# Tiles that matmuls take weights from, padded and moved to multiples of 128 bytes of SBUF

## The chip, the core and the metric

The kernel runs on one NeuronCore of one Trainium2 chip. The metric is the device time of one execution in microseconds (us). Engines are named as in the profile: PE is TensorE (its weight loads stand apart as PEld), DVE VectorE, ACT ScalarE, POOL GpSimd, SP SyncE, whose queue issues most DMAs. SBUF is the on-chip memory with 128 partitions; an offset here is a tile's start address within a partition, modulo 128 bytes.

## What is computed

Three stages run on x of shape (4, 3072, 256), all in float32: a two-dimensional Fourier transform of which the real part is kept, a gated network whose gate mixes all 3072 tokens of a batch, and a second gated network on the 12288 tokens.

```python
x = np.fft.fft(np.fft.fft(x, axis=1), axis=2).real          # (4, 3072, 256)
h = np.maximum(x @ w_in, 0.0)                                # (4, 3072, 1024)
u, v = h[..., :512], h[..., 512:]
v_n = (v - mean(v)) / sqrt(var(v) + 1e-6)                    # over the last axis
v_s = einsum('ts,bsd->btd', w_spatial, v_n) + b_spatial      # (3072 x 3072) per batch
x = ((u * v_s) @ w_out).reshape(12288, 256)
gate = 1 / (1 + exp(-(x @ w_gate)))                          # (12288, 1536)
out = (gate * (x @ w_val)) @ w_out2                          # (12288, 256)
```

## The kernel before

Every product of float32 numbers is made of three matmuls. An operand is split into a high part in the matmul's format float32r and a low part, the rest; `mm3` (lines 256 to 258) issues high x high, high x low and low x high (weights first) into the same PSUM bank. Each of the three has weights of 128 x 128 (the `lhsT` operand, which a weight load brings into the array) and streams 384, 386 or 512 columns of the other operand past them.

- **Transform stage** (to about 310 us). The Fourier transform along the tokens is folded by its symmetries and done as matmuls of folded samples (weights fh, fl, fohl) with cosine and sine tables c1, c2, c3 (streamed), into psf. ACT and DVE take the result into the pairs ph and pl (`take_fft`, line 421). The Fourier transform along the channels and the product with w_in are one product with gc (tiles gh and gl of the pool `keep`) and g3: `v_block` takes weights from ph, pl and nt and streams gc, into psv; `u_block` takes weights from gc and g3 and streams ph, pl and nt, into psu. v is normalized and stored to HBM as v_d, u as u_d. A plan by steps (FOLDS, SPLITS, AT3 and the others) sets the order.
- **Strassen stage** (to about 1827 us). The mixing over tokens runs as Strassen's scheme of seven products, for two pairs of batches and three column blocks: 42 leaves. A leaf is a loop of 6 x 2 x 4 `mm3` with weights from vh, vl and streams from wh, wl, all in pools on the left side of SBUF. DVE and ACT prepare the next tiles three steps ahead (`advance`). DVE takes the four banks into the sums C (`evacuate`), and where a product completes a result it forms the gate g, splits it into gh and gl (here tiles of the pool `gp`), and `second` multiplies that with w_out: two blocks of 12 matmuls, weights woh and wol, streams gh and gl.
- **Gated stage** (to the end). 12 pairs of token blocks by 12 feature blocks, 144 groups. A group forms seven Strassen products with weights wgh, wgl (in the left pools; wg is one tile with both parts) and streams from x tiles: the first seven in the left pool (x0 to x6), then also tail and x7 in tiles of the pool `cp`. `outputs` multiplies the gated result, again tiles gh and gl of `gp`, by weights wv, which lie in `cp`. The order within a group is written by hand: `p12` of group n, `outputs` of n-2, `p34` of n-1, `p67`, `outputs` again, `p5`.

What decides the offsets is the order of allocation. The pools `keep`, `pqp`, `tmp`, `stp`, `vp`, `up` (transform stage), then `cp` and `gp` (later stages) grow from the right end of SBUF toward the left, each below the one before, and a tile is rounded up to a multiple of 32 bytes. `keep` begins with the 28 bytes of masks (line 315), and nt3 has 386 columns, 1544 bytes. The left pools begin at offset 0 and hold tiles of multiples of 128 bytes where matmuls take weights.

```python
masks = keep.tile([P, 3 + B], F32, name="masks")                                                # 315
nts = [keep.tile([P, R3 if unit == 3 else H], F32R, name=f"nt{unit}") for unit in range(4)]     # 318
nn = R3 if q == 0 else H                                                                        # 422
fn = tmp.tile([P, 4, 3 * B], F32, name="fn")                                                    # 480
nt = stp.tile([P, R3], F32R, tag="nt", name="nt", bufs=1)[:, : R3 if unit == 3 else H]          # 588
C = [[cp.tile([P, 4, 512], F32, tag=f"c{k}{c}", name=f"c{k}{c}") for k in range(2)] for c in range(3)]  # 1148
```

Of the kernel before, what the change touches and what calls it, by code (L numbers as in the profile page):

```python
# [9 lines left out]
F32 = mybir.dt.float32  # L10
F32R = mybir.dt.float32r
# [8 lines left out]
B, S, D = 4, 3072, 256  # L20
# [4 lines left out]
P = 128  # L25
H = 384
R3 = H + 2
NT_TOK = B * S


# [13 lines left out]
def _trig(f, num, den):  # L44

    return f(2.0 * np.pi * (np.asarray(num, np.int64) % den) / den)
# [28 lines left out]
def _constants():  # L75
# [15 lines left out]
    c2q = _trig(np.sin, r[:, None] * (2 * i + 1)[None], S // 2)  # L91
    c3p = _trig(np.cos, r[:, None] * np.arange(R3)[None], S // 4)
    c3p[:, H + 1] = 0.0
# [10 lines left out]
def _special_constants():  # L104
# [5 lines left out]
    q2 = _trig(np.sin, s[:, None] * (2 * (2 * j + 1))[None], S)  # L110
    p3 = _trig(np.cos, s[:, None] * (4 * np.arange(R3))[None], S)
    p3[:, H + 1] = 0.0
# [6 lines left out]
SP_P1, SP_Q1, SP_Q2, SP_P3 = 0, H, 2 * H, 3 * H  # L119
SP_N = 3 * H + R3  # L120

# [113 lines left out]
def tile_kernel(ctx: ExitStack, tc: tile.TileContext, t: dict, out: bass.AP):  # L235
# [10 lines left out]
    def f(ap):  # L246
        return ap.bitcast(F32)
# [51 lines left out]
    def pool(stack, name, bufs, side="left", **kw):  # L299
        return stack.enter_context(tc.tile_pool(name=name, bufs=bufs, side=side, reuse_waits="tile", **kw))  # L300
# [3 lines left out]
    keep = pool(r0, "keep", 1, "right")  # L304
# [7 lines left out]
    ps_l = pool(ps0, "ps_l", 1, space=PSUM)  # L312
    ps_w = pool(ps0, "ps_w", 6, space=PSUM)

    masks = keep.tile([P, 3 + B], F32, name="masks")
    gc = [keep.tile([P, 2, DFF], F32R, name=f"g{n}") for n in "hl"]
    g3 = keep.tile([P, DFF], F32R, name="g3")
    nts = [keep.tile([P, R3 if unit == 3 else H], F32R, name=f"nt{unit}") for unit in range(4)]
    sps = cst.tile([P, B + 1, 2, P], F32R, name="sps")
    spc = cst.tile([P, SP_N], F32R, name="spc")  # L320
    cc = {}
# [25 lines left out]
    def folds(eng, parts):  # L347

        a, b = [ALU.add, ALU.subtract], [ALU.subtract, ALU.add]
        for q, e, fo in parts:  # L350
            eng.tensor_tensor(out=e[:, 0:4, :], in0=e[:, 0:4, :], in1=e[:, 4:8, :], op=a[q])
        for q, e, fo in parts:
            eng.tensor_tensor(out=fo[:, 0:2, :], in0=e[:, 0:2, :], in1=e[:, 2:4, :], op=b[q])
        for q, e, fo in parts:
            eng.tensor_tensor(out=e[:, 0:2, :], in0=e[:, 0:2, :], in1=e[:, 2:4, :], op=a[q])
        for q, e, fo in parts:
            eng.tensor_tensor(out=fo[:, 2, :], in0=e[:, 0, :], in1=e[:, 1, :], op=b[q])
        for q, e, fo in parts:
            eng.tensor_tensor(out=fo[:, 3, :], in0=e[:, 0, :], in1=e[:, 1, :], op=a[q])
# [32 lines left out]
    def fft(fold, b, unit, q, e=0, ps=None, tiles=(0, 1, 2), end=True, early=False):  # L392
# [4 lines left out]

        n = R3 if unit == 3 and q == 0 else H
        begin = ps is None
# [19 lines left out]
        return ps, n  # L419

    def take_fft(ps, n, q, p=pqp):
        nn = R3 if q == 0 else H
        hi = p.tile([P, nn], F32R, tag=f"ph{q}", name="ph", bufs=2 if p is pqp else 1)
        lo = p.tile([P, nn], F32R, tag=f"pl{q}", name="pl", bufs=2 if p is pqp else 1)
        nc.scalar.copy(hi[:, :n], ps[:, :n])
        nc.vector.tensor_tensor(out=lo[:, :n], in0=ps[:, :n], in1=f(hi[:, :n]), op=ALU.subtract)
        return hi, lo
# [3 lines left out]
    tmp = pool(s0, "tmp", 1, "right")  # L431
# [13 lines left out]
    def convert(two):  # L445

        new = lambda: tmp.tile([P, 512], F32, tag="cv", name="cv", bufs=5)
        values = from64_rest(from64_first([words[i] for i in two], new), new())
        parts = []
        for i, value in zip(two, values):  # L450
            c, h = pieces[i]
            sl = slice(h * 512, h * 512 + 512)
            hi, lo = (x[:, c, sl] for x in wih)
            nc.scalar.copy(hi, value)
            parts.append((hi, lo, value))

        def rest():
            for hi, lo, value in parts:
                nc.vector.tensor_tensor(out=lo, in0=value, in1=f(hi), op=ALU.subtract)

        return rest
# [15 lines left out]
    xs = tmp.tile([P, B + 1, 2, P], F32, name="xs")  # L477
    nc.sync.dma_start(xs, t["xs"])

    fn = tmp.tile([P, 4, 3 * B], F32, name="fn")  # L480
    folds(nc.gpsimd, [(0, xn, fn)])
    load_table(cst, "c3", {"c3p": (3, R3), "c3q": (3, H)})
    nc.gpsimd.dma_start(spc, t["spc"])
# [4 lines left out]
    rest = convert([0, 1])  # L488
# [51 lines left out]
    rest = convert([2, 3])  # L540
# [23 lines left out]
    take()  # L564
    spread(1)
    pq = [take_fft(*sums[q], q) for q in range(2)]
    load_table(cst, "c1", {"c1": (2, 3, H)})
    mirror_samples(slice(1, B))
# [10 lines left out]
    stp = pool(r0, "stp", 2, "right")  # L579
# [5 lines left out]

    def own_samples(b, unit):

        nt = stp.tile([P, R3], F32R, tag="nt", name="nt", bufs=1)[:, : R3 if unit == 3 else H]
        nc.scalar.activation(nt, f(nts[unit]), AF.Identity, scale=masks[:, 3 + b : 4 + b])
        nt_of[b, unit] = nt  # L590

# [272 lines left out]
    def put_off(step, block=None, also=None):  # L864

        if block is not None:
            seconds[step + LAG] = block()
            if also is not None:
                own_samples(*also)
        if step in seconds:  # L870
            thirds[step + 1] = seconds.pop(step)()
        if step in thirds:
            thirds.pop(step)()

    def transform(at, b, unit, q, to, also):

        found = {}

        def take(values):
            for k, value in enumerate(values):  # L880
                if b == B:
                    take_nyquist(*value, unit + k)
                else:
                    (also if k else to).append(take_fft(*value, q, stp if k else pqp))

        def first():
            found["ps"] = fft(parts_of[b], b, unit, q)
            if unit == 0:
                found["even"] = stp.tile([P, H], F32, tag="even", name="even", bufs=1)
                nc.scalar.copy(found["even"], found["ps"][0][:, :H])  # L890

        def second():
            ps = fft(parts_of[b], b, unit, q, 1, found["ps"][0])[0]
            other = found["even"]
            nc.vector.scalar_tensor_tensor(out=other, in0=other, scalar=2.0, in1=ps[:, :H], op0=ALU.mult, op1=ALU.subtract)
            found["other"] = (other, H)

        if unit == 0:
            ffts.setdefault(at, []).append((first, lambda: None))
            ffts.setdefault(at + 1, []).append((second, lambda: take([found["ps"], found["other"]])))  # L900
        else:
            ffts.setdefault(at, []).append((first, lambda: take([found["ps"]])))

    ffts, pqs = {}, {(0, 3): pq}
    for b in range(B):
# [7 lines left out]
        if b + 1 < B:  # L913
            pqs[b + 1, 3] = []
            for q in range(2):
                transform(base + AT3[q], b + 1, 3, q, pqs[b + 1, 3], None)
    transform(NYQ, B, 0, 0, None, None)
    own_samples(*units[0])
    for (b, unit), follows in zip(units, units[1:] + [None]):
        blocks, later = unit_blocks(pqs[b, unit], b, unit)  # L920
# [21 lines left out]
    cp = pool(ra, "cp", 1, "right")  # L942
# [48 lines left out]
    def evacuate(leaf, ps, d, side):  # L991

        p, i, c = leaf
        s_c, c_c = C[c]
        at = (slice(None), d, slice(None))
# [81 lines left out]
    p, i, c = leaves[-1]  # L1077
# [68 lines left out]
        return raw  # L1146

    C = [[cp.tile([P, 4, 512], F32, tag=f"c{k}{c}", name=f"c{k}{c}") for k in range(2)] for c in range(3)]
    before = None
    first_steps = []  # L1150

    def product(ps, leaf, kp, d):
        p, i, c = leaf
# [6 lines left out]
    for n, leaf in enumerate(leaves[:-1]):  # L1160
        p, i, c = leaf
# [229 lines left out]
```

## Time and profile before

| | |
|---|---|
| time, median of 3 runs | 2944.91 us (2944.33 to 2945.89) |
| the profiled execution | 2942.89 us, its span 2941.1 us |
| granted clock, mean over the span | 0.991 |
| PE busy, share of the span | 97%, 12550 matmuls |
| DVE, ACT, POOL | 69%, 46%, 13% |
| transform stage, to 310.4 us | 1174 matmuls begun |
| from there to 1827 us, Strassen stage | 6600 matmuls, with those on wo |
| gated stage, to the end | the other 4776 matmuls |

A matmul's record lasts longer than its share of the array's time, because matmuls overlap; the pace is the distance between the starts of one and the next, which the timeline gives. Where an engine waits, the profile names what released it. [...]

### The profile page before, as it was taken

What the parts mean: (1) busy time and instruction counts of PE and PEld (TensorE: products, weight loads), DVE (VectorE), ACT (ScalarE), POOL (GpSimd) and SP (SyncE); (2) the same over time, 40 slices, a digit from 0 to 9 for tenths busy, and PEclk for the clock granted to TensorE, in tenths of its full rate; (3) what the DMA queues carried; (4) which work ended last, traced back from release to release, by engine and by line L of the source; (5) the groups of instructions that cost most, each with busy time, mean ns of one, the idle gap of its engine ahead of it and who ended that gap; (6) DMA issues with size and microseconds to landing.
All of it is one profiled execution on the core that took longest, in us unless ns stands there. A gap on an engine that the chain in (4) does not pass through costs nothing.

```text
span 2941.1 us, 34024 instructions
## 1 busy us (share of the span) xinstructions
PE 2863.1 (97%) x12550; PEld 2356.0 (80%) x12550; DVE 2033.2 (69%) x2911; ACT 1338.8 (46%) x2151; POOL 383.2 (13%) x392
## 2 busy tenths in 40 slices
PE   5998899999999999999999999999999999999999
PEld 4887788888888888888887888888888888888887
DVE  7887766777666666577766475866666666666665
ACT  4888433233233232232223233655555555555554
POOL 2882121131112003112001100000000000000000
PEclk8999899999999999999999999999999999999999
DMA  5676875778756677577876473200000000000000
GB/s 224 244 258 238 317 246 204 256 277 307 246 191 232 236 254 233 198 272 256 270 250 229 165 265 132 80 30 29 29 15 15 29 29 29 15 15 29 29 15 15
DMA packets 148136, 470.76 MB, mean 160 GB/s; under 512 B 16753, under 2 KB 18289, under 8 KB 147584
## 3 DMA queue, kind: packets, MB, share of 16 engines
q1 hardware_dynamic: 140528, 434.88, 42.9%
q0 software_dynamic: 3984, 21.11, 1.8%
q10 hardware_dynamic: 3456, 12.58, 1.1%
q8 instruction: 98, 1.61, 0.2%
q14 instruction: 70, 0.57, 0.1%
HBM read 385.94 MB, written 82.58 MB: 159 GB/s over the span
## 4 chain that ended last, share of the span: by engine, by line
PE 90%; DVE 5%; ACT 2%; issue 2%; DMA 1%; POOL 0%; ACTq 0%; DVEq 0%; SPq 0%; POOLq 0%
PE bank L257 28%; PE bank L258 28%; PE bank L256 28%; DVE gl L1028 1%; DMA u_d<-tu 1%; PE psf L256 1%; DVE st L778 1%; DVE g L1020 0%; PE psf L258 0%; PE psf L257 0%; DVE vl L785 0%; PE psv L256 0%; PE psv L257 0%; PE psu L258 0%; PE psu L257 0%
## 5 line engine op out<-in xcount | busy, mean ns | idle before, releaser
L256 PE MATMUL bank<-wh,vh 128*128 128x512 f32 x2016 | 785.6, 390 | 6.7 <-DVE nm L685 6.7
L258 PE MATMUL bank<-wh,vl 128*128 128x512 f32 x2016 | 786.1, 390 | 0.0
L257 PE MATMUL bank<-wl,vh 128*128 128x512 f32 x2016 | 786.0, 390 | 0.0
L785 DVE TENSOR_TENSOR wl<-st,wh 128x1024 fp32r<-128x1024 f32 x252 | 328.3, 1303 | 404.2 <-ACT wh L782 402.4
L782 ACT CAST wh<-st 128x1024 fp32r<-128x1024 f32 x252 | 265.3, 1053 | 611.8 <-PE bank L258 380.0
L256 PEld LDWEIGHTS bank<-wh,vh 128*128 128x128 f32 x2016 | 379.2, 188 | 86.5 <-DVE nm L685 7.4
L257 PEld LDWEIGHTS bank<-wl,vh 128*128 128x128 f32 x2016 | 379.2, 188 | 79.8
L258 PEld LDWEIGHTS bank<-wh,vl 128*128 128x128 f32 x2016 | 379.0, 188 | 79.4
L1274 DVE TENSOR_TENSOR t<-t,bank 128x512 f32<-128x512 f32 x144 | 98.9, 687 | 250.8 <-PE bank L258 250.7
L257 PE MATMUL bank<-x,wgh 128*128 128x512 f32 x673 | 265.8, 395 | 0.0
L258 PE MATMUL bank<-x,wgl 128*128 128x512 f32 x673 | 265.6, 395 | 0.0
L256 PE MATMUL bank<-x,wgh 128*128 128x512 f32 x673 | 264.0, 392 | 0.4 <-ACT t L1286 0.4
L778 POOL TENSOR_TENSOR st<-st 128x1024 f32<-128x1024 f32 x60 | 158.5, 2642 | 812.8 <-DMA st<-v_d 695.5
L778 DVE TENSOR_TENSOR st<-st 128x1024 f32<-128x1024 f32 x180 | 225.5, 1253 | 40.7 <-DMA st<-in_wt 40.3
L1295 DVE TENSOR_TENSOR gl<-s,gh 128x512 fp32r<-128x512 f32 x288 | 199.3, 692 | 57.4 <-ACT gh L1293 44.4
L256 PE MATMUL bank<-gh,wv 128*128 128x512 f32 x576 | 226.8, 394 | 0.8 <-ACT gh L1288 0.8
L258 PE MATMUL bank<-gh,wv 128*128 128x512 f32 x576 | 227.6, 395 | 0.0
L257 PE MATMUL bank<-gl,wv 128*128 128x512 f32 x576 | 225.8, 392 | 0.2 <-DVE gl L1295 0.2
L1265 ACT ACTIVATE s<-s 128x512 f32<-128x512 f32 x144 | 91.0, 632 | 148.6 <-DVE s L1264 148.6
L256 PEld LDWEIGHTS bank<-x,wgh 128*128 128x128 f32 x673 | 126.4, 188 | 31.3 <-ACT t L1286 0.8
L257 PEld LDWEIGHTS bank<-x,wgh 128*128 128x128 f32 x673 | 126.2, 188 | 30.6
L258 PEld LDWEIGHTS bank<-x,wgl 128*128 128x128 f32 x673 | 126.2, 188 | 28.6
(233 smaller groups left out, 4537.9 us busy)
## 6 DMA issues: line engine op xcount, KB each, us to landing
st<-in_wt SPq DMA_DIRECT2D x432, 512.0 KB, 5.2
st<-v_d SPq DMA_DIRECT2D x144, 512.0 KB, 4.8
u<-u_d SPq DMA_DIRECT2D x96, 256.0 KB, 4.2
u_d<-tu SPq DMA_DIRECT2D x48, 384.0 KB, 3.7
v_d<-tv SPq DMA_DIRECT2D x69, 256.0 KB, 2.8
xt<-in_xh SPq DMA_DIRECT2D x24, 512.0 KB, 4.5
x_d<-x ACTq DMA_DIRECT2D x24, 512.0 KB, 2.8
raw<-x_d SPq DMA_DIRECT2D x24, 512.0 KB, 4.1
```

Of the source, the lines that this page charges most:

```text
L256: nc.tensor.matmul(out=ps, lhsT=w[0], rhs=x[0], start=first, stop=False, **kw)
L257: nc.tensor.matmul(out=ps, lhsT=w[0], rhs=x[1], start=False, stop=False, **kw)
L258: nc.tensor.matmul(out=ps, lhsT=w[1], rhs=x[0], start=False, stop=last, **kw)
L778: (nc.gpsimd if kind == "v" else nc.vector).tensor_tensor(out=tiles[0], in0=tiles[0], in1=tiles[1], op=ALU.add if sign > 0 else ALU.subtract)
L782: nc.scalar.copy(hl[0], tiles[0])
L785: lows.append(lambda: nc.vector.tensor_tensor(out=hl[1], in0=tiles[0], in1=f(hl[0]), op=ALU.subtract))
L1028: side["low"] = lambda: nc.vector.tensor_tensor(out=gl, in0=g, in1=f(gh), op=ALU.subtract)
L1265: nc.scalar.activation(s1, s1, AF.Sigmoid)
L1274: nc.vector.tensor_tensor(out=g["t2"], in0=g["t2"], in1=g["b"], op=ALU.add)
L1295: nc.vector.tensor_tensor(out=l, in0=s, in1=f(h), op=ALU.subtract)
```

## The change

It pads or moves tiles. RP is R3 (386 columns) rounded up to a multiple of 32 columns, 416. ph, pl for q = 0 and the tile nt of `stp` get RP columns; matmuls use as much of them as before. masks is allocated after gc, g3 and nts, with 16 columns of which 7 are used; fn gets 64 columns of which 48 are used. A tile "rest" of 96 bytes, never written, stands after C, so that `gp` begins 96 bytes further left. An unused name goes.

```diff
--- before.py
+++ after.py
@@ -25,6 +25,9 @@
 P = 128
 H = 384
 R3 = H + 2
+
+ROW = 32
+RP = -(-R3 // ROW) * ROW
 NT_TOK = B * S
 
 
@@ -312,10 +315,10 @@
     ps_l = pool(ps0, "ps_l", 1, space=PSUM)
     ps_w = pool(ps0, "ps_w", 6, space=PSUM)
 
-    masks = keep.tile([P, 3 + B], F32, name="masks")
     gc = [keep.tile([P, 2, DFF], F32R, name=f"g{n}") for n in "hl"]
     g3 = keep.tile([P, DFF], F32R, name="g3")
     nts = [keep.tile([P, R3 if unit == 3 else H], F32R, name=f"nt{unit}") for unit in range(4)]
+    masks = keep.tile([P, 16], F32, name="masks")[:, : 3 + B]
     sps = cst.tile([P, B + 1, 2, P], F32R, name="sps")
     spc = cst.tile([P, SP_N], F32R, name="spc")
     cc = {}
@@ -419,7 +422,7 @@
         return ps, n
 
     def take_fft(ps, n, q, p=pqp):
-        nn = R3 if q == 0 else H
+        nn = RP if q == 0 else H
         hi = p.tile([P, nn], F32R, tag=f"ph{q}", name="ph", bufs=2 if p is pqp else 1)
         lo = p.tile([P, nn], F32R, tag=f"pl{q}", name="pl", bufs=2 if p is pqp else 1)
         nc.scalar.copy(hi[:, :n], ps[:, :n])
@@ -477,7 +480,7 @@
     xs = tmp.tile([P, B + 1, 2, P], F32, name="xs")
     nc.sync.dma_start(xs, t["xs"])
 
-    fn = tmp.tile([P, 4, 3 * B], F32, name="fn")
+    fn = tmp.tile([P, 2 * ROW], F32, name="fn")[:, : 12 * B].rearrange("p (s k) -> p s k", s=4)
     folds(nc.gpsimd, [(0, xn, fn)])
     load_table(cst, "c3", {"c3p": (3, R3), "c3q": (3, H)})
     nc.gpsimd.dma_start(spc, t["spc"])
@@ -585,7 +588,7 @@
 
     def own_samples(b, unit):
 
-        nt = stp.tile([P, R3], F32R, tag="nt", name="nt", bufs=1)[:, : R3 if unit == 3 else H]
+        nt = stp.tile([P, RP], F32R, tag="nt", name="nt", bufs=1)[:, : R3 if unit == 3 else H]
         nc.scalar.activation(nt, f(nts[unit]), AF.Identity, scale=masks[:, 3 + b : 4 + b])
         nt_of[b, unit] = nt
 
@@ -1146,8 +1149,9 @@
         return raw
 
     C = [[cp.tile([P, 4, 512], F32, tag=f"c{k}{c}", name=f"c{k}{c}") for k in range(2)] for c in range(3)]
+
+    cp.tile([P, 24], F32, name="rest")
     before = None
-    first_steps = []
 
     def product(ps, leaf, kp, d):
         p, i, c = leaf
```

In the built program, these are the offsets, in bytes past a multiple of 128:

| tiles | used as | before | after |
|---|---|---|---|
| vh, vl, wh, wl, wgh, wgl, wg, x0 to x6 | weights and streams | 0 | 0 |
| fh, fl, fohl, sps | weights of psf | 0 | 0 |
| c1, c2, c3 (parts of tables) | streams of psf | 32 to 96 | the same |
| gc, g3, nts | weights of psu, streams of psv | 64 | 0 |
| ph, pl | weights of psv, streams of psu | 0, 32, 64 or 96 | 0 |
| nt | weights of psv, streams of psu | 64 | 0 |
| fd, wih, wil | first product | 96 | 0 |
| woh, wol, gh, gl of `gp` | weights and streams of `second` | 96 | 0 |
| wv, tail, x7 (in tiles of C) | weights and streams of the gated stage | 96 | 0 |

The fourth window of a block of unit 3 (columns 258 to 385) begins 8 bytes past the offset of its tile, before and after. On every engine the same instructions stand in the same order; one wait differs, that of the first DVE instruction that writes a tile tv, which no longer waits for a DMA.

## Rows read from the trace of the kernel before

**Rows 1.** Page, section 4: the chain that ended last, by engine.

```profile
PE 90%; DVE 5%; ACT 2%; issue 2%; DMA 1%; POOL 0%; ACTq 0%; DVEq 0%; SPq 0%; POOLq 0%
```

**Rows 2.** Busy time by stage: length, PE, PEld, DVE, ACT, POOL (instructions), granted clock, DMA.

```profile
0.00:310.40 310.40, 249.13 (x1174) 220.20 (x1175) 253.15 (x634) 228.66 (x458) 173.15 (x271) 0.93 0.67 243
...
335.00:1827.00 1492.00, 1487.33 (x6536) 1226.12 (x6535) 1005.21 (x1088) 443.48 (x519) 202.77 (x108) 1.00 0.70 239
1850.00:2930.00 1080.00, 1080.00 (x4658) 873.76 (x4657) 734.01 (x1124) 632.71 (x1122) 0.00 (x0) 1.00 0.07 25
```

**Rows 3.** Grouped rows by shape: count, busy us, mean ns, idle before.

```profile
L256 PE MATMUL bank<-wh,vh 128*128 128x512 f32 x2016 | 785.6, 390 | 6.7 <-DVE nm L685 6.7
...
L258 PE MATMUL bank<-gh,wv 128*128 128x512 f32 x576 | 227.6, 395 | 0.0
...
L257 PE MATMUL bank<-gl,woh 128*128 128x512 f32 x184 | 73.1, 397 | 4.7 <-DVE gl L1028 4.7
...
L256 PEld LDWEIGHTS bank<-wh,vh 128*128 128x128 f32 x2016 | 379.2, 188 | 86.5 <-DVE nm L685 7.4
...
L256 PEld LDWEIGHTS bank<-gh,wv 128*128 128x128 f32 x576 | 108.1, 188 | 26.5 <-ACT gh L1288 1.2
```

**Rows 4.** Timeline (start us, us), PE, Strassen stage, 1000 to 1003 us.

```profile
1000.05 0.39 PE L258 MATMUL bank<-wh,vl 128*128 128x512 f32 x1
...
1002.77 0.39 PE L258 MATMUL bank<-wh,vl 128*128 128x512 f32 x1
```

**Rows 5.** Timeline, PE, one period of the gated stage.

```profile
2502.72 0.39 PE L256 MATMUL bank<-x,wgh 128*128 128x512 f32 x1
...
2503.19 0.39 PE L258 MATMUL bank<-x,wgl 128*128 128x512 f32 x1
...
2506.89 0.39 PE L256 MATMUL bank<-x,wgh 128*128 128x512 f32 x1
...
2510.37 0.39 PE L256 MATMUL bank<-x,wgh 128*128 128x512 f32 x1
```

**Rows 6.** Timeline, weight loads, 1830 to 1840 us, offset 96 then 0.

```profile
1831.70 0.19 PEld L258 LDWEIGHTS bank<-tail,wol 128*128 128x128 f32 x1
...
1835.10 0.19 PEld L258 LDWEIGHTS bank<-tail,wol 128*128 128x128 f32 x1
...
1837.64 0.19 PEld L257 LDWEIGHTS bank<-x,wgh 128*128 128x128 f32 x1
...
1839.91 0.19 PEld L258 LDWEIGHTS bank<-x,wgl 128*128 128x128 f32 x1
```

**Rows 7.** Timeline, PE, from the Strassen stage into the gated stage.

```profile
1826.21 0.39 PE L256 MATMUL bank<-wh,vh 128*128 128x512 f32 x1
...
1827.80 0.39 PE L257 MATMUL bank<-x,wgh 128*128 128x512 f32 x1
```

**Rows 8.** Timeline, ACT, in the same period as rows 5.

```profile
2505.01 0.59 ACT L1286 COPY t<-bank 128x512 f32<-128x512 f32 x1 [0.73 <-PE bank L258]
```

**Rows 9.** Timeline, PE, around one block of 12 on wo.

```profile
1020.45 0.39 PE L258 MATMUL bank<-wh,vl 128*128 128x512 f32 x1
...
1026.21 0.39 PE L256 MATMUL bank<-wh,vh 128*128 128x512 f32 x1
```

**Rows 10.** Transform stage: timeline, PE; then grouped rows of 18 to 310 us.

```profile
301.43 0.40 PE L257 MATMUL psv<-gl,ph 128*128 128x512 f32 x1
...
302.83 0.34 PE L256 MATMUL psu<-ph,gh 128*128 128x384 f32 x1
...
304.59 0.34 PE L649 MATMUL psu<-nt,g 128*128 128x384 f32 x1
...
L256 PE MATMUL psu<-ph,gh 128*128 128x384 f32 (+1 forms) x128 | 45.9, 359 | 3.1 <-ACT eu L651 3.1
...
L256 PE MATMUL psv<-gh,ph 128*128 128x512 f32 x100 | 41.1, 411 | 1.1 <-ACT ev L624 1.0
...
L617 PE MATMUL psv<-g,nt 128*128 128x512 f32 x52 | 23.0, 442 | 17.8 <-ACT nt L589 17.8
```

## The prediction

> **What bounds the kernel now.** The page's chain of waits comes first [rows 1]: 90% of the chain that ended last lies on TensorE (PE), so what its matmuls cost decides, provided that nothing else comes late. The table by stage shows where this is strict [rows 2]. In the transform stage (to 310 us) PE is busy 249 of 310 us and waits for ACT and DVE. In the Strassen stage (335 to 1827 us) it is busy 1487.3 of 1492.0 us, and in 1080 us of the gated stage all of them, with 4658 matmuls in 1080.00 us: 231.9 ns from one start to the next. [...]
>
> The grouped rows hide why [rows 3]. A weight load has a recorded 188 ns whether its tile begins at a multiple of 128 bytes (wh,vh: weights vh) or 96 bytes past one (gh,wv: weights wv). By durations of records this change is worth nothing. The matmul means differ a little: 390 ns for wh,vh in the Strassen stage, 395 ns for gh,wv in the gated one. These are durations of overlapping work; what counts is start to start, and for that the timeline is the view.
>
> In the Strassen stage, where weights and streamed tiles all begin at offset 0 (of 128 bytes), 12 starts take 2.72 us [rows 4]: 226.7 ns each. In the gated stage weights (wgh, wgl at 0; wv at 96) and streams (x at 0 or 96; tail, gh, gl at 96) alternate. One period of the loop has 33 matmuls, 2502.72 to 2510.37 us: 7.65 us, 231.8 ns each [rows 5]. Both are 512 columns wide. The question is whether offsets make the 5.1 ns.
>
> The beginning of the gated stage answers it nearly by itself. From 1830 us on the second product of the last leaf runs 24 matmuls with weights wo and stream tail, all at 96. Its settled part has 15 loads from 1831.70 to 1835.10 us, 226.7 ns each. Then come wgh and x, at 0. The next 11 take 2.54 us, 230.9 ns each, and the 10 after that 2.27 us, 227.0 ns again [rows 6]. So a steady offset of 96 costs nothing, a change of offset costs some 11 x 4.2 = 47 ns, spread over ten matmuls. A change of tiles with no change of offset costs nothing: from vh to wgh, other pools, other products, the pace from 1826.21 to 1827.80 us is 7 starts in 1.59 us, 227 ns [rows 7]. In the gated period an offset changes every three to six matmuls, before the pace has settled.
>
> **The change part by part.** It moves no instruction and adds none; every tile that matmuls take weights from, and nearly every one they stream, then begins at 0. Only the DFT tables, streamed, keep their offsets, and the last window of seven-block units begins 8 bytes past. One wait of one early DVE instruction on a DMA falls away; that instruction still waits for ACT, and the change of wait is taken as nothing.
>
> Gated stage: 4658 matmuls x 226.7 ns = 1055.8 us instead of 1080.0, so 24.2 us less, and 0.2 for the rest of the stage. About ten real waits there would each still leave a transient of 0.05 us: 0.5 at most. I take **24.2 us**. The cover must last: PE then takes 0.17 us less per period. The nearest producer is ACT's copy t (L1286), which ends at 2505.60 us, while the matmul that overwrites its bank starts at 2506.89 us [rows 5, 8]: 1.29 us of slack, seven times what is needed. If it gave out, the wait would hand back the part of the 0.17 us that exceeds it, so 24 us at the very most.
>
> Strassen stage: only the second matmul of finished products leaves offset 0 (wo, gh, gl at 96). From the last start before such a block to the start 25 matmuls later, 1020.45 to 1026.21 us, are 5.76 us instead of 25 x 226.7 = 5.67 [rows 9]: 0.1 us. The 552 matmuls on wo there (three groups of 184, one of them in [rows 3]) are 46 blocks of 12: 4.6 us. Some blocks also wait for gl, 4.7 us in all [rows 3], and keep a transient after that: **4.3 us**.
>
> Transform stage: weights here begin at 64, 32 or 96 and the width alternates between 384 and 512. Six starts at 512 columns take 1.40 us (233 ns), 10 at 384 columns 1.76 us (176 ns) [rows 10]. [...] Nothing is the other end; I take **1.0 us**. [...]
>
> Sum: 24.2 + 4.3 + 1.0 = 29.5 us. The profiled execution took 2942.89 us (span 2941.1), so 2913.4; the median is 2.0 us above it, so 2944.91 - 29.5 = **2915.4 us**, 1.0% faster.
>
> The pace of [rows 6] reacts to a change between offsets 96 and 0, both multiples of 32 bytes. [...]
>
> **The rivals.** *No change, 2944.9 us.* The 5.1 ns come from something else that the gated stage has and the Strassen stage has not, such as ACT and DVE reading PSUM beside PE all the time; offsets then only happen to change where tiles change, and multiples of 32 bytes are as good as those of 128. For: ACT is busier there. Against: after 1837.64 us the settled pace holds in the same stage, and the wo blocks are disturbed in the Strassen stage too, where ACT is busy 443 of 1492 us [rows 2, 9]. 5%.
>
> *Half the gain, about 2930 us.* Offsets are one cause, and the frequent change of tile and product another. For: the settled pace is on record only for runs in which few kinds of tile alternate. Against: vh to wgh. 14.5 us would be left. 7%.
>
> *Slower.* Weights and stream that begin at the same offset meet at the same place of SBUF in every matmul, and the pace locks to its worst value instead of its best; the worst two in a row that I see take 0.47 us, 2502.72 to 2503.19 us, 235 ns each [rows 5]. From a settled pace of 231.9 ns on it is slower than before; at 235 ns, 4658 x 3.1 ns = 14 us more: 2959 us. Against: the Strassen stage has both at offset 0 and settles at 226.7. 2%.
>
> **How the numbers follow.** Forecast 86%, half 7%, nothing 5%, slower 2%. The forecast's own bounds are 24.4 + 4.6 + 3.5 + 3 = 35.5 and 23.7 + 4 + 0 - 3 = 24.7 us of gain: 2909.4 to 2920.2; with a little of the half case above, 2908 to 2923 holds 8 in 10. A measurement here can tell about 0.2%, 6 us, from no change. Faster 0.93, same 0.05, slower 0.02.
>
> **What would show it.** In the profile after, a period of 33 matmuls takes 7.48 us and the mean of gh,wv falls from 395 to about 390 ns, while weight loads stay at 188 ns; the wo blocks take 5.67 us per 25. The Strassen pace stays 226.7. Wrong would be: a gated pace still near 232 ns (the first rival), 229 (the second), a new PE wait on ACT t or DVE gl in the gated stage, or a clock under 1.00 after 335 us.

## The result and the profile after

| | before | after |
|---|---|---|
| median, 4 runs each (lowest to highest) | 2945.40 us (2944.33 to 2946.22) | 2918.62 us (2917.74 to 2919.96) |
| the profiled execution, its span | 2942.89, 2941.1 us | 2919.47, 2917.7 us |
| transform stage, first matmul to the first of the next stage | 293.0 us | 292.4 us |
| Strassen stage, the same | 1516.5 us | 1517.6 us |
| gated stage, to the last matmul | 1109.9 us | 1085.7 us |

The ratio of the medians is 0.991, with a 95% interval of 0.9893 to 0.9927: 26.8 us less, where 29.5 were forecast. The stages are taken from the starts of matmuls, in one profiled execution of each kernel. In these two the whole gain lies in the gated stage; the Strassen stage, where 4.3 us of gain had been expected, takes 1.1 us more.

The page's chain by engine, which answers to [rows 1]: PE still leads, with 87% instead of 90%; DVE's share has grown from 5% to 6%. The line of DVE that makes gl stands in it with 1%, as it did before.

```profile
PE 87%; DVE 6%; ACT 2%; issue 2%; POOL 1%; DMA 1%; ACTq 0%; DVEq 0%; POOLq 0%
PE bank L260 28%; PE bank L261 28%; PE bank L259 28%; DVE st L781 1%; DVE gl L1031 1%; DMA u_d<-tu 1%; DVE g L1023 1%; ACT wh L785 1%; DVE vl L788 0%; PE psf L259 0%; DVE stats L642 0%; DVE wl L788 0%; PE psf L261 0%; PE psf L260 0%; PE psv L259 0%
```

The table by stretches (length, busy time and count of PE, PEld, DVE, ACT and POOL, then granted clock, DMA share and GB/s), which answers to [rows 2]. In 1050 us of the gated stage stand 4632 matmuls, 226.7 ns each. The kernel before has 4528 in the same stretch, 231.9 ns each. In the Strassen stage PE is busy 1484.8 us, 2.5 less than before.

```profile
0.00:310.40 310.40, 245.90 (x1175) 217.34 (x1176) 254.93 (x635) 228.27 (x458) 174.07 (x272) 0.95 0.66 244
335.00:1827.00 1492.00, 1484.83 (x6531) 1227.33 (x6530) 1004.47 (x1087) 443.42 (x518) 205.35 (x108) 1.00 0.70 239
1850.00:2900.00 1050.00, 1049.98 (x4632) 868.84 (x4631) 729.08 (x1119) 629.10 (x1117) 0.00 (x0) 1.00 0.07 25
```

The grouped rows (instructions by line and tile: busy us, mean ns of one, idle time before them), which answer to [rows 3]; lines have moved by three. The mean of gh,wv (L258 before, L261 now) has fallen from 395 to 389 ns, the one of wh,vh stands at 390, the weight loads stay at 188.

```profile
L259 PE MATMUL bank<-wh,vh 128*128 128x512 f32 x2016 | 786.6, 390 | 6.7 <-DVE nm L688 6.7
L261 PE MATMUL bank<-gh,wv 128*128 128x512 f32 x576 | 224.1, 389 | 0.0
L259 PEld LDWEIGHTS bank<-wh,vh 128*128 128x128 f32 x2016 | 379.8, 188 | 86.5 <-DVE nm L688 7.4
L259 PEld LDWEIGHTS bank<-gh,wv 128*128 128x128 f32 x576 | 108.1, 188 | 23.7 <-ACT gh L1292 1.2
```

The timeline of PE over one period of the gated loop, which answers to [rows 5]: from the first to the last row are 33 matmuls, 7.48 us, where 7.65 stood.

```profile
2502.61 0.39 PE L259 MATMUL bank<-gh,wv 128*128 128x512 f32 x1
2502.84 0.39 PE L260 MATMUL bank<-gl,wv 128*128 128x512 f32 x1
...
2510.09 0.39 PE L259 MATMUL bank<-gh,wv 128*128 128x512 f32 x1
```

The timeline of weight loads where the blocks on wo end and those on wgh begin, which answers to [rows 6]: the 11 loads from the second row to the third take 2.50 us, 227.3 ns each. The transient of 2.54 us is gone.

```profile
1835.18 0.19 PEld L261 LDWEIGHTS bank<-tail,wol 128*128 128x128 f32 x1
1836.08 0.19 PEld L259 LDWEIGHTS bank<-x,wgh 128*128 128x128 f32 x1
...
1838.58 0.19 PEld L261 LDWEIGHTS bank<-x,wgl 128*128 128x128 f32 x1
```

A block on wo inside the Strassen stage, which answers to [rows 9]: the last start before it and the start 25 matmuls later, 5.67 us apart instead of 5.76.

```profile
1021.13 0.39 PE L261 MATMUL bank<-wh,vl 128*128 128x512 f32 x1
1021.36 0.39 PE L259 MATMUL bank<-gh,woh 128*128 128x512 f32 x1
...
1026.80 0.39 PE L259 MATMUL bank<-wh,vh 128*128 128x512 f32 x1
```

So the blocks on wo gained what was forecast, and yet the stage as a whole did not. The waits of PE in the stage say why: 7.2 us for gl, where before 4.7 stood [rows 3].

```profile
PE bank L260 <- DVE gl L1031: 7.2, 6, 2.9
```

One of the six, around 828 us, in the timelines of PE, DVE and POOL. DVE's split of gl, 0.68 us in the median, takes 2.83 us: it stands beside a sum on POOL that began 0.60 us earlier, and ends 0.55 us after it. PE stands still for it, and then its starts are 0.43 us apart instead of 0.227: the second fence gives a granted clock of 0.51 for that stretch, and 0.50 behind another of the six.

```profile
828.29 2.83 DVE L1031 TENSOR_TENSOR gl<-g,gh 128x512 fp32r<-128x512 f32 x1
827.69 2.88 POOL L781 TENSOR_TENSOR st<-st 128x1024 f32<-128x1024 f32 x1 [2.75 <-DMA st<-v_d]
831.18 0.79 PE L260 MATMUL bank<-gl,woh 128*128 128x512 f32 x1 [2.36 <-DVE gl L1031]
831.77 0.63 PE L261 MATMUL bank<-gh,wol 128*128 128x512 f32 x1
832.20 0.63 PE L259 MATMUL bank<-wh,vh 128*128 128x512 f32 x1
```

```profile
830.80:834.30 3.50, 3.12 (x7) 2.48 (x8) 1.76 (x3) 1.86 (x3) 0.00 (x0) 0.51 0.87 329
1588.60:1592.00 3.40, 3.40 (x10) 2.63 (x9) 2.15 (x3) 2.47 (x3) 0.00 (x0) 0.50 0.75 299
```

The same place of the kernel before, in the timelines of DVE and POOL: there the sum on POOL begins 0.05 us after gl, and it is the next instruction of DVE, vl, that takes 3.43 instead of 1.21 us. Nobody on PE waits for that one yet.

```profile
829.98 0.68 DVE L1028 TENSOR_TENSOR gl<-g,gh 128x512 fp32r<-128x512 f32 x1
830.58 3.43 DVE L785 TENSOR_TENSOR vl<-st,vh 128x1024 fp32r<-128x1024 f32 x1
830.03 2.90 POOL L778 TENSOR_TENSOR st<-st 128x1024 f32<-128x1024 f32 x1 [3.40 <-DMA st<-v_d]
```

After the change two of the waits (at 828 and 1585 us, 2.75 and 3.33 us from start to start) are followed by the lower clock, before none (the longest pause is 2.23 us, at 1585 us, where a long gl stood beside a sum on POOL already). What the long distances in the stage cost over the settled pace, summed from the starts that are more than 0.26 us apart, is 6.3 us before and 11.8 us after: 2.5 us more waiting, 3.0 us at half clock.

### The profile page after: what moved, and what is told of

It reads as the page before. It is cut to its first block, busy times and chain, and to the rows that moved or that the text cites. A ratio compares the mean times of both kernels' runs of the same rounds, so it can differ in the third digit from the quotient of the medians.

```text
span 2917.7 us, 34024 instructions
## 1 busy us (share of the span) xinstructions
PE 2833.9 (97%) x12550; PEld 2354.9 (81%) x12550; DVE 2032.4 (70%) x2911; ACT 1338.2 (46%) x2151; POOL 386.4 (13%) x392
## 4 chain that ended last, share of the span: by engine, by line
PE 87%; DVE 6%; ACT 2%; issue 2%; POOL 1%; DMA 1%; ACTq 0%; DVEq 0%; POOLq 0%
PE bank L260 28%; PE bank L261 28%; PE bank L259 28%; DVE st L781 1%; DVE gl L1031 1%; DMA u_d<-tu 1%; DVE g L1023 1%; ACT wh L785 1%; DVE vl L788 0%; PE psf L259 0%; DVE stats L642 0%; DVE wl L788 0%; PE psf L261 0%; PE psf L260 0%; PE psv L259 0%
## 5 line engine op out<-in xcount | busy, mean ns | idle before, releaser
L261 PE MATMUL bank<-wh,vl 128*128 128x512 f32 x2016 | 786.0, 390 | 0.0
L261 PEld LDWEIGHTS bank<-wh,vl 128*128 128x128 f32 x2016 | 379.7, 188 | 78.8
L261 PE MATMUL bank<-x,wgl 128*128 128x512 f32 x673 | 261.8, 389 | 0.0
L259 PE MATMUL bank<-gh,wv 128*128 128x512 f32 x576 | 224.2, 389 | 0.8 <-ACT gh L1292 0.8
L261 PE MATMUL bank<-gh,wv 128*128 128x512 f32 x576 | 224.1, 389 | 0.0
L261 PEld LDWEIGHTS bank<-x,wgl 128*128 128x128 f32 x673 | 126.3, 188 | 26.3
```

Of the source, the lines that this page charges most:

```text
L259: nc.tensor.matmul(out=ps, lhsT=w[0], rhs=x[0], start=first, stop=False, **kw)
L261: nc.tensor.matmul(out=ps, lhsT=w[1], rhs=x[0], start=False, stop=last, **kw)
```

## The experiments

The pace in the gated stage is given as matmuls in the 1050 us from 1850 us on; the excess is (1050 us / count - 1050 us / 4632) x 4776 matmuls. Times are set against the kernel before in runs beside them, whose median lay between 2945.4 and 2949.4 us.

| run | offsets in the later stages | time, us | ratio, 95% | matmuls | excess, us |
|---|---|---|---|---|---|
| before | left 0, right 96 | | | 4528 | 24.9 |
| after | all 0 | 2918.62 | 0.991 [0.9893, 0.9927] | 4632 | 0 |
| e1_late_only | all 0 | 2918.84 | 0.9902 [0.9887, 0.9917] | 4632 | 0 |
| e2_early_only | as before | 2947.80 | 0.9997 [0.9988, 1.0007] | 4529 | 24.6 |
| e3_all_96 | all 96 | 2919.71 | 0.9904 [0.9887, 0.992] | 4632 | 0 |
| e4_right_64 | left 0, right 64 | 2938.95 | 0.9971 [0.9962, 0.9981] | 4553 | 18.8 |
| e5_right_32 | left 0, right 32 | 2941.53, one run | | 4541 | 21.7 |
| e6_weights_96 | wv 96, else 0 | 2934.80, one run | | 4575 | 13.5 |
| e7_streams_96 | gh, gl, wo 96, else 0 | 2940.01, one run | | 4552 | 19.0 |
| e9_mixed | Strassen: weights 0, streams 96; gated: x0 to x6, wg and the last three of the ten pairs wgh, wgl 96, else 0 | 2979.83, one run | | 4536 | 22.9 |
| e11_lagged, e12_block_96 | wv, gh, gl, wo 96, else 0 | 2943.47, 2937.65, one run each | | 4553, 4568 | 18.8, 15.2 |

**Which edit.** The first run has the kernel before with the tile "rest" and nothing else; the second the changed kernel without it.

```diff
+    cp.tile([P, 24], F32, name="rest")
```

> The kernel before with only the 96-byte tile after C: the tiles of the pools cp and gp (wo, wv, gh, gl, tail, x7) begin at offset 0, those of the transform stage stay at 32, 64 or 96. Theory (changes of offset cost pace in the Strassen and gated stages alone): gated pace 226.7 ns, 33 matmuls in 7.48 us as in the changed kernel, blocks on wo without the 0.1 us, so 24 + 4 us less than before, within 3 us of the changed kernel's 2918.6 us. Rival (the transform stage's offsets carry a part of the gain): more than 3 us above the changed kernel, up to the 3.5 us bound of the prediction.

> The changed kernel without the 96-byte tile: only the transform stage's tiles begin at 0, the later pools are at 96 again. Theory: the gated pace is 231.8 ns again and the time that of before, 2945 us, less at most 1 us. Rival (offsets of the transform stage matter): 2941 to 2943 us, with Strassen and gated stages as before.

The 96 bytes bring everything that can be measured. The other edits (masks, fn, and RP for nt, ph and pl) are worth 0.9 us by the ratio, with an interval from 3.5 us of gain to 2.1 us of loss.

**Multiples of 128, or one common offset.** The kernel before with a tile of 96 bytes ahead of the left pools of the later stages (in front of `A["v"]`), so that everything there lies at 96:

```diff
+        pool(la, "lead", 1).tile([P, 24], F32, name="lead")
         A["v"] = pool(la, "vr", 7)
```

> The kernel before with a tile of 96 bytes ahead of the left pools of the Strassen and gated stages, so that every weight and stream of both stages begins at offset 96, none at a multiple of 128. Theory A (only a change of offset between successive matmuls costs): 226.7 ns everywhere in both stages, about 28 us less than before, 2917 to 2920 us. Theory B (what counts is that a tile begins at a multiple of 128 bytes): every matmul of both stages pays what those at 96 pay, 226.7 + 5 ns or more, so 2945 us plus some 6000 x 5 ns = 30 us, 2975 us.

The stretch of 1050 us in the gated stage:

```profile
1850.00:2900.00 1050.00, 1049.92 (x4632) 868.82 (x4631) 728.95 (x1119) 629.23 (x1118) 0.00 (x0) 1.00 0.07 25
```

4632 matmuls, as many as at offset 0. Multiples of 128 bytes are not what counts; that all tiles share one offset is enough.

**How far apart.** "rest" of 32 and of 64 bytes in place of 96, put into the kernel before, bring the right pools to 64 (e4) and to 32 (e5, with [P, 16]); the diff of e4 against e1:

```diff
-    cp.tile([P, 24], F32, name="rest")
+    cp.tile([P, 8], F32, name="rest")
```

> The kernel before with a tile of 32 bytes after C: the later right-hand pools begin at offset 64, the left ones at 0. If the unit is 128 bytes, offsets 0 and 64 alternate in the gated stage and disturb the pace as 0 and 96 did: 231 to 232 ns, time near 2945 us. If the unit is 64 bytes, 0 and 64 are the same: 226.7 ns and 2917 to 2920 us. If the cost goes with the distance to the unit, something between.

> The kernel before with a tile of 64 bytes after C: the later right-hand pools begin at offset 32, the left ones at 0. With 96 the gated stage had 24.8 us over the pace of 226.7 ns, with 64 (e4) 18.6 us. If only the change counts and not its size: 18 to 25 us here too. [...] If the cost falls with the distance from 0 downward: under 15 us.

Every difference that was tried costs: 18.8 us at 64, 21.7 at 32, 24.9 at 96.

**Weights or streams.** In the changed kernel, "rest" between the tiles c0 and c1 moves only wv to 96; a pool of 32 bytes between `cp` and `gp` moves only gh, gl and wo.

```diff
-    C = [[cp.tile([P, 4, 512], F32, tag=f"c{k}{c}", name=f"c{k}{c}") for k in range(2)] for c in range(3)]
-
+    C = [[cp.tile([P, 4, 512], F32, tag=f"c0{c}", name=f"c0{c}")] for c in range(3)]
     cp.tile([P, 24], F32, name="rest")
+    for c in range(3):
+        C[c].append(cp.tile([P, 4, 512], F32, tag=f"c1{c}", name=f"c1{c}"))
```

```diff
     cp = pool(ra, "cp", 1, "right")
+    pool(ra, "shift", 1, "right").tile([P, 8], F32, name="shift")
     gp = pool(ra, "gp", 1, "right")
```

> The changed kernel with the 96 bytes between the tiles c0 and c1 of C: in the gated stage wv (weights) begins at 96, every other weight and every stream at 0. Two changes to 96 and two back per period of 33 matmuls, in the weights alone. If weight loads are what is disturbed: most of the 24 us is back, 15 us or more over the changed kernel's gated stage of 1085.7 us. If the streams are: within 1 us of 1085.7.

> The changed kernel with a tile of 32 bytes between the pools cp and gp: gh and gl begin at 96, so that in the gated stage the streams alone change offset, at the same four places per period, with all weights at 0 (in the Strassen stage the blocks on wo have weights and streams at 96, as before the change). If streams are what is disturbed: 15 us or more over 1085.7. If weight loads alone are: within 1 us of it, and the wo blocks cost 4 us as before.

Both cost, 13.5 and 19.0 us, the first less than was expected of weights as the only cause; neither the weights alone nor the streams alone are the cause. The second of these runs holds something better than its total. The last 24 matmuls on wo have weights at 96 and their stream, tail, at 0, one after the other. In the timeline of PE:

```profile
1832.91 0.39 PE L260 MATMUL bank<-tail,woh 128*128 128x512 f32 x1
...
1838.04 0.40 PE L261 MATMUL bank<-tail,wol 128*128 128x512 f32 x1
```

These are 22 starts in 5.13 us, 233.2 ns each, and the pace doesn't come down. In the kernel before the same block, with both at 96, ran at 226.7 [rows 6].

**A standing difference.** In the changed kernel the tile of 96 bytes stands between the pools of v and w, so that in the whole Strassen stage weights lie at 0 and streams at 96, with no change from one matmul to the next.

```diff
         A["v"] = pool(la, "vr", 7)
+        pool(la, "lead", 1).tile([P, 24], F32, name="lead")
         A["w"] = pool(la, "wr", 4)
```

> The changed kernel with 96 bytes between the pools of v and w on the left: through the whole Strassen stage all weights (vh, vl) begin at 0 and all streams (wh, wl) at 96, with no change between successive matmuls except at the blocks on wo (both at 0). In the gated stage weights and streams change often. e6 and e7 left open whether the change or the mixture costs, since their 6 matmuls on wv were mixed throughout. Theory (the change costs): a settled pace of 226.7 ns in the Strassen stage, the stage 4 us longer at most for its 46 blocks; the gated stage 12 to 25 us longer than 1085.7. Rival (weights and streams at different offsets cost on every matmul): 231 ns or more in the Strassen stage, 6048 x 4.3 ns = 26 us or more there.

The timeline of PE in a quiet stretch: nine starts in 2.10 us, 233.3 ns each.

```profile
600.15 0.39 PE L259 MATMUL bank<-wh,vh 128*128 128x512 f32 x1
600.38 0.39 PE L260 MATMUL bank<-wl,vh 128*128 128x512 f32 x1
600.61 0.40 PE L261 MATMUL bank<-wh,vl 128*128 128x512 f32 x1
...
602.25 0.39 PE L259 MATMUL bank<-wh,vh 128*128 128x512 f32 x1
```

The stage takes 1554.0 us instead of 1517.6. Here the theory that only a change of offset costs anything falls: a difference that stands still costs 6.6 ns in every matmul.

**Which pair must agree.** If it were only a matmul's own weights and stream (theory D), moving all of wv, gh and gl to 96 would cost nothing. If it were the stream of one matmul and the weights of the next, whose load begins within 0.01 us of it (timelines of PE and PEld after the change, 1000 to 1002.5 us; theory C), then the first weights and the last stream of each block would have to come from offset 0. e12 has the two edits of e6 and e7 together; e11 has them too, and the following, which leaves out a part of the products on wv:

```diff
-            mm3(po[k][o], wv(fb, o), G[n]["g"][k], fb == 0, fb == 11)
+            (wh, wl), (gh, gl) = wv(fb, o), G[n]["g"][k]
+            w0 = wg(fb, "a11")[0] if o == 0 else wh
+            x0 = xs_[j, "t1"][0] if o == 1 else gh
+            nc.tensor.matmul(out=po[k][o], lhsT=w0, rhs=gh, start=fb == 0, stop=False)
+            nc.tensor.matmul(out=po[k][o], lhsT=wh, rhs=gl, start=False, stop=False)
+            nc.tensor.matmul(out=po[k][o], lhsT=wl, rhs=x0, start=False, stop=fb == 11)
```

> e9 showed a steady cost where all weights are at 0 and all streams at 96, so it is not the change alone. In the traces the weight load of matmul i+1 begins as matmul i begins to stream. Theory C: a pair costs where the stream of one matmul and the weights of the next lie at different offsets. Here the two blocks of 6 matmuls on wv per period are arranged so that no such pair differs: wv, gh, gl at 96, everything else of the gated stage at 0, but the first matmul of a block takes weights of wgh (0) and streams gh (96), the last takes weights wv (96) and streams an x tile (0). The offset still changes four times a period, and two matmuls of a block have weights and stream at different offsets. This leaves out a part of the products on wv (two of six factors are other tiles), with the same count and shape of matmuls. Theory C: gated stage 1085.7 us within 1.5 us, 226.7 ns throughout. Theory A (a change of offset costs): 10 us or more above it. Theory D (a matmul's own weights and stream must agree): also 10 us or more.

> The control of e11: the same offsets (wv, gh, gl at 96, the rest of the gated stage at 0) with the operands of the changed kernel. Each matmul's own weights and stream agree, but entering a block the stream before it (0) meets weights at 96, and leaving it the stream gh (96) meets weights at 0: four differing pairs a period instead of twelve in e6 and e7. Theories A and C: the pace is disturbed at each of these, 8 to 25 us above 1085.7. Theory D (own weights and stream must agree): within 1.5 us of 1085.7.

The gated stretch of e11 and of e12:

```profile
1850.00:2900.00 1050.00, 1050.00 (x4553) 854.27 (x4551) 719.05 (x1104) 621.53 (x1102) 0.00 (x0) 1.00 0.07 26
```

```profile
1850.00:2900.00 1050.00, 1050.00 (x4568) 857.66 (x4567) 720.62 (x1106) 623.24 (x1108) 0.00 (x0) 1.00 0.07 26
```

Neither pair alone will do: 18.8 and 15.2 us of excess. With own pairs in agreement throughout the loop (e12), the four changes of offset per group still cost 15.2 us / (144 x 4) = 26 ns each. So both a standing difference (e9) and a change (e12, [rows 6]) cost, and of what was tried on 128x512 matmuls only one offset for everything is free. A change always brings a stream and the next weights at different offsets, so these runs don't separate the two: that either pair costs when it differs would fit all of them as well. Why the pace depends on offsets stays open.

**What the Strassen stage lost.** The offsets alone don't decide how long PE waits for gl there. The profile of e2, whose later stages have the offsets of before, shows the 7.2 us of the changed kernel and two falls of the clock (first line); the profile of e1, with the offsets of after, shows 4.0 us and one fall (second line).

```profile
PE bank L260 <- DVE gl L1031: 7.2, 5, 3.0
PE bank L257 <- DVE gl L1028: 4.0, 3, 2.9
```

Over all profiles with the sums on POOL these waits lie between 3.3 us (e9) and 9.2 us (e6). With one profile of each kernel it stays open whether kernels or executions differ. Two runs then test the collision itself: the changed kernel, and the kernel before, with the sums of v on DVE instead of POOL:

```diff
-            (nc.gpsimd if kind == "v" else nc.vector).tensor_tensor(
+            nc.vector.tensor_tensor(
```

> The changed kernel with the 60 sums of the tiles v moved from POOL to DVE, which adds 60 x 1.25 = 75 us to DVE's 2032. In the changed kernel PE waited 7.2 us for gl in the Strassen stage instead of 4.7, and one gl of 0.68 us took 2.83 us while POOL's sum ran (827.69 to 830.57 us). Theory (the two engines keep each other out, and the residue of the gain went there): no DVE instruction on 128x512 over 1 us, waits for gl under 4 us, no clock below 1.00 after 335 us, 2 to 5 us less than the changed kernel. Rival: the sums wait in DVE's queue for their DMAs ahead of gl and the evictions, the waits grow over 10 us and the time by as much.

> The kernel before with the 60 sums of the tiles v on DVE instead of POOL, offsets as before. In e8 the same edit took all waits for gl out of the Strassen stage. Theory (two independent costs): the Strassen stage loses its 4.7 us of waits for gl and what the clock lost after them, the gated stage stays at 1109.9 us with its pace of 231.8 ns, and the time lies some 6 to 10 us under that of before. Rival (the waits exist only because PE got ahead): no change against before.

| | time, us | ratio to before, 95% |
|---|---|---|
| e8_sums_on_dve | 2909.45 | 0.987 [0.9854, 0.9887] |
| e10_before_dve | 2937.55 | 0.9966 [0.9954, 0.9979] |

The table of e8 by stretches, and a sum of v and gl from DVE's timeline:

```profile
335.00:1820.00 1485.00, 1485.00 (x6551) 1229.13 (x6550) 1014.18 (x1150) 447.15 (x520) 45.30 (x48) 1.00 0.71 241
```

```profile
828.84 1.22 DVE L781 TENSOR_TENSOR st<-st 128x1024 f32<-128x1024 f32 x1
829.97 1.22 DVE L788 TENSOR_TENSOR wl<-st,wh 128x1024 fp32r<-128x1024 f32 x1
831.11 0.68 DVE L1031 TENSOR_TENSOR gl<-g,gh 128x512 fp32r<-128x512 f32 x1
```

The instructions that make the tile gl between 335 and 1820 us (least, median and greatest ns), of the kernel before, of the changed kernel and of e8:

```profile
L1028 DVE TENSOR_TENSOR gl<-g,gh x92: 676/683/2922, 454.8 to 1805.9; 128x512 fp32r<-128x512 f32 x92
```

```profile
L1031 DVE TENSOR_TENSOR gl<-g,gh x92: 675/685/2895, 454.4 to 1806.9; 128x512 fp32r<-128x512 f32 x92
```

```profile
L1031 DVE TENSOR_TENSOR gl<-g,gh x92: 679/683/692, 458.4 to 1799.3; 128x512 fp32r<-128x512 f32 x92
```

None takes longer than 692 ns any more. DVE makes a sum in 1.22 us, POOL took 2.88 for the one shown above, and PE waits for nothing in 1485 us, nor in e10. The collision with POOL is thereby shown as the cause of the waits for gl and of the two falls of the clock. This version is the fastest, 9.2 us below the changed kernel by the medians, more than was expected; in the profiled executions 7.5 us (2919.47 to 2911.94), of which the stage gives 11.1 (1517.6 to 1506.5) while the transform stage takes 3.0 us more, a size by which it varies among runs (291.3 to 295.5). In the kernel before the same edit is worth 11.0 us by the medians. The two gains add up, 26.8 + 11.0 = 37.8 against the 37.0 of both edits together (2946.45 to 2909.45), closer than the medians of before lie to each other: offsets and collisions are separate costs.

## Why the prediction held, step by step

- **What bounds it, and the reading of the weight loads.** Right. The durations of weight loads (188 ns before and after) showed nothing, the distances of starts everything.
- **Gated stage, 24.2 us.** Right: 24.1 us between the stages, by the starts. The cover lasted; PE is busy 1049.98 of the 1050 us, so ACT's t and DVE's gl cost nothing there.
- **Strassen stage, 4.3 us.** The mechanism was right, the term was not. The excess of the starts at pace (less than 0.26 us apart) fell by 4.3 us, from 4.5 to 0.2 over the stage, as worked out. The step that failed is the one on the waits: the prediction named the 4.7 us that some blocks wait for gl and took them as fixed but for a transient after them. They are not fixed. In the profile after, gl begins at 828 us 0.60 us behind a sum on POOL instead of 0.05 us ahead of one, and the pause at 1585 us has grown; over the stage the waits grew by 2.5 us and brought 3.0 us at half clock. Net: -1.1 us. Since e2 shows the same loss with the offsets of before, it is a spread of the waits, for which the range had no room, and not shown to be a price of the change. The list of wrong signs held it in two parts, "a new PE wait on DVE gl", though only for the gated stage, and "a clock under 1.00 after 335 us", which came.
- **Transform stage, 1.0 us.** 0.6 us by the stage times. No run shows the 1.0 us as a term, nor the 3.5 and the 3 us that stand for this stage in the bounds; what the two profiles show in their place is this. Of the starts that are less than 0.26 us apart, those at 512 columns in psv stand 232.8 ns apart before and 231.2 after (means of 306 and 309), those at 384 columns in psu 175.9 and 175.7 (of 334 and 343), though nearly all weights and streams of psv and psu now share an offset. The widths still alternate there, but no run separates widths from offsets. At a granted clock of 0.50 the starts are 427 ns apart at 512 columns and 320 at 384, before and after, and the granted clock of the first 310.4 us is 0.93 before and 0.95 after. e2 bounds all edits there to between 3.5 us of gain and 2.1 us of loss: not to be told from nothing.
- **Sum.** 24.1 - 1.1 + 0.6 = 23.6 us against 23.4 in the profiled executions, which is less than the 24.7 of the prediction's own lower bound. By the medians it is 26.8, inside the range; for the 96 bytes alone (e1) it is 30.6, against the kernel before in runs beside it (2949.43 to 2918.84). The profiled execution of before, 2942.89 us, was 1.4 us shorter than the shortest of its four timed ones, and the one of after was one of its two longer ones (2919.47 and 2919.96 against 2917.78 and 2917.74). What sets these apart wasn't profiled, and that the measured median lies inside the range in spite of the waits is in part luck.
- **The rivals.** No change: false, by the result and by e1, where the 96 bytes alone bring the gain; nor are multiples of 32 bytes as good as one common offset (e4, e5). Half the gain: false, since no disturbance is left in the gated stage at one offset, however often tiles and products change. Slower, by the same offset in weights and stream: false, and its opposite true; the same offset is the free case, and a differing one locks at 233.3 ns (e9), near the 235 ns that the rival had named as the worst.
- **The mechanism as told.** "A steady offset of 96 costs nothing, a change of offset costs some 47 ns" stood on [rows 6], where weights and stream are both at 96. e3 bears it out. It was incomplete: it doesn't say that a steady difference between the two costs 6.6 ns in every matmul (e9), and the loop before has such matmuls too, those on wgh and wgl at 0 that stream tail or x7 at 96. In e12, where the next change comes after 6 to 12 matmuls, a change costs 26 ns and not 47. The sum didn't need either, because it compared two paces and the change removes both costs.

## What to carry to other kernels

Where PE has no gaps, read its pace from starts, over a block of one kind and across the borders of blocks; here a few ns per matmul showed there and not in the durations of weight loads. Where 128x512 matmuls bound the time as here, try one offset for all tiles that they read: one filler tile of 96 bytes was worth 1.0% (e1), and 96 for all did as well as 0 for all. Before the time of a stage is forecast to a few us, look at the waits in it and at what DVE and POOL run side by side: the waits for gl varied from profile to profile by more than the forecast for the stage, and went only when the sums left POOL (e8, e10).

## What was not expected of the hardware

- A 128x512 matmul with its weight load settles at 226.7 ns where all offsets agree (0 or 96), and runs at 231.9 on average where they alternate between 0 and 96 as in this loop, and at 233.3 where weights and stream differ steadily, in either direction (weights 0 and streams 96 in e9, the reverse in e7).
- A DVE instruction of 0.68 us took 2.83 us, and one of 1.21 us took 3.43, beside a sum of 2.9 us on POOL: the first ended 0.55 us after the sum and the second 1.08 us after it. Between 335 and 1820 us of the two profiles ten gl took 2.82 to 2.92 us, each beside such a sum. They began 0.03 to 0.88 us behind its start, and all of them ended 0.55 us after its end, so they were held until the sum was through and not slowed in part. With the sums on DVE no gl took more than 692 ns (e8). What holds them is not shown.
- Pauses of PE of 2.75 and 3.33 us from start to start were followed by granted clocks of 0.51 and 0.50 in the stretches shown, with 1.4 and 1.6 us lost against the pace; after the one of 2.23 us in the kernel before it stayed at 1.00.
